# The output accumulator of a decode kernel as two column groups of one bank, with a column-split closing copy and two stores

## The chip, the cores and the metric

The kernel runs on one core of one Trainium2 chip. The metric is device time in microseconds (us) of one execution, as the median of several.

PE is the matmul engine (PEld its weight loads), DVE is VectorE, ACT is ScalarE, POOL is GpSimd, SP is the queue that issues most DMAs. A name like DVEq or SPq is the instruction queue of that engine.

## The reference, cut to what matters

One token for each of four batch rows. A is attention over the last 2048 positions of a cache with 16 key/value heads and 32 query heads; B is a small MLP. The output is 4 rows of 576 numbers.

```python
xn = _layernorm(x)                               # x: (4, 1, 576)
out = x + A(xn, k_cache, v_cache, wq, wo) + B(xn, w1, w2, w3, w4)
# A: q = xn @ wq; softmax(q k^T) v; then  o(4, 4096) @ wo(4096, 576)
# B with S = 1: the shifted terms are zero, so B = xn + gelu(layernorm(xn) @ w3) @ w4,  w4(4608, 576)
```

All three summands end in the same four rows, so the kernel adds them in one accumulator in PSUM, the memory that matmuls write: first `x + xn`, then 32 terms of the wo projection in four groups of eight, then 36 terms of w4. A term is one 128-row slice of the contraction: 128x4 weights against 128x576 moving data.

## The kernel before: the parts that the change touches

The accumulator is one bank of PSUM, and its matmuls take the 576 columns as two halves of `CW` = 288. The kernel before stacks the halves as extra rows. The 4-column weights (`gT`, `op`) lie in a zeroed tile at every second column, 10 wide. A slice of 8 columns that starts at column 1 or at column 0 puts the four batch rows in the even or in the odd output rows and adds zero to the others. Eight rows `(b i)` are thus a contiguous image of the output, and one store writes it.

```python
NI = 2; CW = D // NI                         # 288 columns
OR = NI * B; OW = OR + NI                    # 8 rows, 10-wide padded weights
ROWS = slice(NI - 1, NI - 1 + OR, NI)
gT = cleared([P, NF, OW], "gT")              # zeroed by ACT; data goes to [:, :, ROWS]
op = cleared([P, WOR, OW], "op")
acc = ps_acc.tile([P, CW], F32)              # one PSUM bank
nc.vector.memset(acc[:], 0.0)
second = []

def acc_matmuls(terms):
    for i in range(NI):
        for n, (lhsT, rhs) in enumerate(terms):
            # odd terms go to another bank, at rows 32 to 39, once `second` is set
            to, q, start = (second[0], QD, second[1]) if second and n % 2 else (acc, 0, False)
            nc.tensor.matmul(out=to[q:q + OR, :], lhsT=lhsT[:, NI - 1 - i:NI - 1 - i + OR],
                             rhs=rhs[:, i * CW:(i + 1) * CW], start=start, stop=False, skip_group_check=True)
            if start:
                second[1] = False
```

Before the last wo projection `second` is set. From there even terms go to rows 0 to 7 of `acc` and odd terms to rows 32 to 39 of `acc_odd`, which is another bank. `acc_matmuls` is called for two terms at a time, so neighbours alternate between the banks and run at the same time: in the trace the two of a pair start within 0.01 us of each other, and the pairs are 0.12 us apart at full clock. The w4 matrix arrives in six loads. The last two, of one term each, are summed into `acc` alone, so that ACT can copy `acc_odd` out meanwhile:

```python
W4_PIECES = [0, NFH, NF - 12, NF - 6, NF - 2, NF - 1, NF]     # 0 18 24 30 34 35 36
...
second += [acc_odd, True]
... # o_turn, o_sum, o_spread, o_pick of the last head
o_proj(hl)                                   # 8 terms of wo
mlp_out(*pieces[0]) ... mlp_out(*pieces[3])  # 34 terms of w4
second.clear()
odd = const.tile([OR, CW], F32)
nc.scalar.activation(out=odd[:], in_=acc_odd[QD:QD + OR, :], func=ACT.Copy)
seen = const.tile([1, 1], F32)
nc.vector.tensor_copy(out=seen[:], in_=odd[0:1, 0:1])
for lo, hi in pieces[4:]:                    # terms 34 and 35
    mlp_out(lo, hi)

fin = const.tile([OR, CW], out.dtype)
nc.vector.tensor_tensor(out=fin[:], in0=acc[0:OR, :], in1=odd[:], op=ALU.add)
nc.sync.dma_start(out=o2.rearrange("b (i n) -> (b i) n", i=NI), in_=fin[:])
```

## Time and profile before

| | before |
|---|---|
| median of 3 runs | 211.74 us (211.57 to 211.84) |
| span of the profiled execution | 209.9 us |
| load queue q1 | 87.17 MB, 97.5% of the 16 DMA engines' span |
| PE, DVE busy | 71%, 54% of the span |

The page of the profile, cut to the lines that say what bounds the kernel: busy time of PE, two rows in 40 equal slices of the span (DMA share in tenths, memory traffic), the load queue with its packets, megabytes and share, and the chain of waits by engine.

```profile
span 209.9 us, 2326 instructions
PE 149.1 (71%) x941; PEld 60.2 (29%) x955; DVE 113.7 (54%) x165; ACT 34.4 (16%) x66; POOL 8.9 (4%) x33
...
DMA  8999999999999999999999999999999999999991
GB/s 294 406 403 440 422 428 431 437 425 432 448 429 419 421 437 421 447 418 437 434 425 437 418 426 439 434 423 440 418 431 437 422 433 431 434 428 446 417 399 71
...
q1 hardware_dynamic: 6640, 87.17, 97.5%
...
DMA 52%; PE 24%; DVE 19%; issue 2%; ACT 1%; SPq 0%; DVEq 0%; ACTq 0%
```

The DMA row is 9 in every slice but the first and the last. The stream of loads never pauses, and the last slice is what happens behind it. That slice is where the change acts, so here are its instructions from the timeline (start, duration, engine, line, operation, shapes, count, and in brackets the idle time before and what ended it). In this timeline, lines that don't matter to the point are left out, weight loads above all:

```profile
194.51 1.05 PE L394 MATMUL O<-vn,PT 128*32 128x512 bf16 x16 [0.62 <-DMA vn<-in_A_v_cache_dram]
...
200.70 0.40 PE L183 MATMUL acc<-w_sb,gT 128*8 128x288 bf16 x1 [0.78 <-DMA w_sb<-in_B_w_dram]
...
206.60 0.65 PE L183 MATMUL acc<-w_sb,gT 128*8 128x288 bf16 x4
206.81 0.40 ACT L612 ACTIVATE odd<-acc_odd 8x288 f32<-8x288 f32 x1 [10.46 <-PE acc_odd L183]
207.25 0.14 DVE L614 COPY seen<-odd 1x1 f32<-1x1 f32 x1 [8.54 <-ACT odd L612]
207.32 0.43 DVE L619 TENSOR_TENSOR fin<-acc,odd 8x288 bf16<-8x288 f32 x1
207.78 0.37 SPq L620 DMA_DIRECT2D out_dram<-fin  x1
```

PE starts w4 when its first piece lands. It works off the last four matmuls, two halves of two terms, one after the other from 206.60 and ends at 206.60 + 0.65 = 207.25. Then come one adding copy of 0.43 us, the issue of the store at 207.78, and 2.1 us until the span ends. From the semaphore events of the trace, the six pieces of w4 landed at 200.65, 202.57, 204.69, 206.07, 206.43 and 206.81 us. The end of the kernel can therefore be cut in three:

- **last landing to PE end**: 207.25 - 206.81 = 0.44 us
- **PE end to store issue**: 207.78 - 207.25 = 0.53 us
- **store issue to span end**: 209.89 - 207.78 = 2.11 us

Together they are 3.08 us.

### The profile page before, as it was taken

To read this page: it belongs to the slowest core of one execution; us is meant where nothing else is said; L and a number is where in the kernel's file an instruction comes from. 1 tells how busy PE (TensorE), PEld (TensorE's weight loads), DVE (VectorE), ACT (ScalarE), POOL (GpSimd) and SP (SyncE) were. 2 spreads that over 40 slices of the span, in tenths; PEclk is the share of its full clock that TensorE was granted. 3 is DMA by queue.
4 is the path that set the end of the run, shared out by engine and by line. 5 is a ranking of instruction groups with operands and counts; after the bars stand their busy time and mean duration, and the time that the engine had idled before them with its cause. 6 is when DMAs were issued, how large, how long until landed. Compare 5 with 4: busy or idle time off the path is not lost.

```text
span 209.9 us, 2326 instructions
## 1 busy us (share of the span) xinstructions
PE 149.1 (71%) x941; PEld 60.2 (29%) x955; DVE 113.7 (54%) x165; ACT 34.4 (16%) x66; POOL 8.9 (4%) x33
## 2 busy tenths in 40 slices
PE   0378198699670039649998999659995976898684
PEld 0123032233220013223454333224331312343353
DVE  3611877985910084917507898465949391755200
ACT  7612201021120001111120312110111111113100
POOL 4620000000000000000000300000000000000000
PEclk9999769999996557976999999999997968899969
DMA  8999999999999999999999999999999999999991
GB/s 294 406 403 440 422 428 431 437 425 432 448 429 419 421 437 421 447 418 437 434 425 437 418 426 439 434 423 440 418 431 437 422 433 431 434 428 446 417 399 71
DMA packets 6658, 87.31 MB, mean 416 GB/s; under 512 B 748, under 2 KB 1016, under 8 KB 1656
## 3 DMA queue, kind: packets, MB, share of 16 engines
q1 hardware_dynamic: 6640, 87.17, 97.5%
q8 instruction: 7, 0.11, 0.2%
q10 hardware_dynamic: 8, 0.00, 0.0%
q14 instruction: 3, 0.02, 0.0%
HBM read 87.17 MB, written 0.00 MB: 415 GB/s over the span
## 4 chain that ended last, share of the span: by engine, by line
DMA 52%; PE 24%; DVE 19%; issue 2%; ACT 1%; SPq 0%; DVEq 0%; ACTq 0%
DMA vn<-in_A_v_cache_dram 19%; DMA w_sb<-in_B_w_dram 15%; DVE kt L226 14%; DMA kn<-in_A_k_cache_dram 12%; PE S L342 9%; DMA wq_sb<-in_A_wq_dram 6%; PE acc L183 4%; PE O L394 2%; PE g_ps L460 2%; PE q_ps L286 2%; DVE mx L348 2%; PE S L364 1%; PE oT L407 1%; DVE PT L376 1%; DVE dm L350 1%
## 5 line engine op out<-in xcount | busy, mean ns | idle before, releaser
L342 PE MATMUL S<-kt,qz 128*128 128x512 bf16 x242 | 74.0, 429 | 34.5 <-DVE kt L226 31.3
L226 DVE STREAM_TRANSPOSE kt<-kn 128x2048 int32<-128x2048 int32 x32 | 73.4, 2295 | 26.5 <-DMA kn<-in_A_k_cache_dram 25.0
L342 PEld LDWEIGHTS <-qz 128*128 128x128 bf16 x256 | 24.0, 108 | 63.5 <-issue 46.6
L394 PE MATMUL O<-vn,PT 128*32 128x512 bf16 x256 | 22.9, 400 | 8.4 <-DMA vn<-in_A_v_cache_dram 8.4
L370 ACT ACTIVATE E<-S 128x512 bf16<-128x512 f32 x16 | 9.5, 597 | 97.7 <-PE S L364 97.7
L376 DVE STREAM_TRANSPOSE PT<-E 128x512 bf16<-128x512 bf16 x16 | 11.4, 710 | 15.5 <-ACT E L370 15.5
L401 ACT ACTIVATE O_sb<-O,rd 128x512 f32<-128x512 f32 x16 | 11.0, 686 | 37.1 <-PE O L394 37.1
L394 PEld LDWEIGHTS <-PT 128*32 128x32 bf16 x256 | 5.9, 94 | 29.6 <-issue 28.6
L417 DVE TENSOR_REDUCE on<-oT 128x8 bf16<-128x128 f32 x16 | 4.6, 287 | 16.7 <-PE oT L407 16.6
L348 DVE TENSOR_REDUCE mx<-S 128x1 f32<-128x512 f32 x16 | 10.5, 658 | 1.2 <-PE S L342 1.1
L407 PE MATMUL oT<-ident_w,O_sb 128*128 128x128 f32 x64 | 11.0, 296 | 0.3 <-ACT O_sb L401 0.3
L407 PEld LDWEIGHTS oT<-ident_w,O_sb 128*128 128x128 f32 x64 | 7.0, 146 | 4.6 <-issue 3.9
L183 PE MATMUL acc<-wo_sb,op 128*8 128x288 bf16 x56 | 7.5, 286 | 1.0 <-DVE op L439 1.0
L364 PE MATMUL S<-nm,j_row 8*128 8x512 bf16 x16 | 6.3, 393 | 1.9 <-DVE nm L360 1.7
L183 PE MATMUL acc<-w_sb,gT 128*8 128x288 bf16 x38 | 6.6, 342 | 0.8 <-DMA w_sb<-in_B_w_dram 0.8
L380 PE MATMUL dn<-rs,same_j 128*128 128x1 f32 x32 | 6.4, 268 | 0.0
L380 PEld LDWEIGHTS dn<-rs,same_j 128*128 128x128 f32 x32 | 5.2, 204 | 4.1 <-issue 3.4
L330 PE MATMUL S<-negbig,ohT 4*128 4x512 bf16 x16 | 6.1, 384 | 0.0
L183 PE MATMUL acc_odd<-w_sb,gT 128*8 128x288 bf16 x34 | 6.1, 350 | 0.0
L183 PEld LDWEIGHTS <-op 128*8 128x8 bf16 x64 | 4.6, 87 | 3.2 <-DVE op L439 1.1
L286 PE MATMUL q_ps<-wq_sb,xnT 128*32 128x512 bf16 x40 | 4.5, 630 | 1.3 <-DMA wq_sb<-in_A_wq_dram 1.3
L478 DVE COPY g_x<-gT_ps 128x64 f32<-128x64 f32 (+1 forms) x3 | 0.6, 194 | 8.5 <-PE gT_ps L472 8.5
(93 smaller groups left out, 80.7 us busy)
## 6 DMA issues: line engine op xcount, KB each, us to landing
kn<-in_A_k_cache_dram SPq DMA_DIRECT2D x16, 2048.0 KB, 23.8
vn<-in_A_v_cache_dram SPq DMA_DIRECT2D x16, 2048.0 KB, 25.6
wo_sb<-in_A_wo_dram SPq DMA_DIRECT2D x4, 1152.0 KB, 26.4
w_sb<-in_B_w_dram SPq DMA_DIRECT2D x1, 4608.0 KB, 33.2
wq_sb<-in_A_wq_dram SPq DMA_DIRECT2D x1, 4096.0 KB, 12.8
w_sb<-in_B_w_dram SPq DMA_DIRECT2D x1, 2592.0 KB, 32.2
w_sb<-in_B_w_dram SPq DMA_DIRECT2D x2, 864.0 KB, 34.0
w_sb<-in_B_w_dram SPq DMA_DIRECT2D x2, 576.0 KB, 32.5
```

Source lines behind the costliest of these rows:

```text
L183: nc.tensor.matmul(out=to[q:q + OR, :], lhsT=lhsT[:, NI - 1 - i:NI - 1 - i + OR], rhs=rhs[:, i * CW:(i + 1) * CW], start=start, stop=False ...
L226: nc.vector.transpose(out=kt[:], in_=src)
L286: nc.tensor.matmul(out=q_ps[r][g * QD:(g + 1) * QD, :], lhsT=xnT[:, k, :], rhs=wq_sb[:, col:col + NW], start=(j == 0), stop=False, skip_gr ...
L342: nc.tensor.matmul(out=S_ps[h][:], lhsT=qz[:, z0:z0 + P], rhs=kt[:, ib, c0:c0 + SC, e:2 * QD:2].rearrange("p c k -> p (c k)"), start=False ...
L348: nc.vector.reduce_max(out=mx[:], in_=S_ps[h][:], axis=AX.X)
L364: nc.tensor.matmul(out=S_ps[h][:], lhsT=j_row[:], rhs=st.pop(("nm", h))[:, 0:1].to_broadcast([NJ, NW]), start=False, stop=False, skip_grou ...
L370: nc.scalar.activation(out=E[h][:].rearrange("p c k -> p (c k)"), in_=S_ps.pop(h)[:], func=ACT.Exp, scale=scale, accum_out=rs[:])
L376: nc.vector.transpose(out=PT[h][:], in_=E.pop(h)[:])
L380: nc.tensor.matmul(out=dn[:], lhsT=same_j[:], rhs=st.pop(("rs", h))[:], start=True, stop=True)
L394: nc.tensor.matmul(out=O_ps[h][g * QD:(g + 1) * QD], lhsT=PT[h][:, c, :], rhs=vn[:, :, c, :], start=(s == 0), stop=False, skip_group_check ...
L401: nc.scalar.activation(out=O_sb[h][:], in_=O_ps.pop(h)[:], func=ACT.Copy, scale=st.pop(("rd", h))[:, 0:1])
L407: nc.tensor.transpose(out=oT[:, s, :], in_=o[:, s, :], identity=ident_w[:, s * NJ:s * NJ + P])
```

## The change

The intent is to drop the padded weights and the second bank. Column half `i` of every term goes to partitions 32·i to 32·i+3 of the one accumulator bank, called column group `i` of PE here, so each term is a pair of matmuls that is meant to run at the same time, in the body too. The closing eviction needs no addition, so it is split by columns over DVE and ACT. As the halves are no longer neighbouring rows, there are two stores, on two queues. Two loads of w4 are merged into one.

```diff
-    W4_PIECES = [0, NFH, NF - 12, NF - 6, NF - 2, NF - 1, NF]
+    W4_PIECES = [0, NFH, NF - 6, NF - 2, NF - 1, NF]
...
-    gT = cleared([P, NF, OW], "gT")
-    op = cleared([P, WOR, OW], "op")
+    gT = const.tile([P, NF, B], BF16, name="gT")
+    op = const.tile([P, WOR, B], BF16, name="op")
...
     def acc_matmuls(terms):
-        for i in range(NI):
-            for n, (lhsT, rhs) in enumerate(terms):
-                ... (as printed above)
+        for lhsT, rhs in terms:
+            for i in range(NI):
+                nc.tensor.matmul(out=acc[i * QD:i * QD + B, :], lhsT=lhsT, rhs=rhs[:, i * CW:(i + 1) * CW],
+                                 start=False, stop=False, skip_group_check=True)
...
-    mlp_out(*pieces[0])
-    ... (acc_odd, second, odd, seen: all gone)
+    for lo, hi in pieces:
         mlp_out(lo, hi)
-    fin = const.tile([OR, CW], out.dtype)
-    nc.vector.tensor_tensor(out=fin[:], in0=acc[0:OR, :], in1=odd[:], op=ALU.add)
-    nc.sync.dma_start(out=o2.rearrange("b (i n) -> (b i) n", i=NI), in_=fin[:])
+    fin = const.tile([P, CW], out.dtype)
+    nc.vector.tensor_copy(out=fin[:, 0:CW // 2], in_=acc[:, 0:CW // 2])
+    nc.scalar.activation(out=fin[:, CW // 2:], in_=acc[:, CW // 2:], func=ACT.Copy)
+    for i, eng in enumerate((nc.sync, nc.scalar)):
+        eng.dma_start(out=o2[:, i * CW:(i + 1) * CW], in_=fin[i * QD:i * QD + B, :])
```

Cut: the same reshaping where `op` and `gT` are written, the loops that called `acc_matmuls` for two terms at a time, and the small padded identity `idz` for the first term.

More of the change, by code (lines that the diff above doesn't have):

```diff
@@ L166 @@
     qz = cleared([P, ZP + Hkv * 4 * P], "qz")
-    OR = NI * B
-    OW = OR + NI
-    ROWS = slice(NI - 1, NI - 1 + OR, NI)
-    gT = cleared([P, NF, OW], "gT")
-    op = cleared([P, WOR, OW], "op")
+    gT = const.tile([P, NF, B], BF16, name="gT")
+    op = const.tile([P, WOR, B], BF16, name="op")
     acc = ps_acc.tile([P, CW], F32)
     nc.vector.memset(acc[:], 0.0)
-    second = []
     def acc_matmuls(terms):
-        for i in range(NI):
-            for n, (lhsT, rhs) in enumerate(terms):
-                to, q, start = (second[0], QD, second[1]) if second and n % 2 else (acc, 0, False)
-                nc.tensor.matmul(out=to[q:q + OR, :], lhsT=lhsT[:, NI - 1 - i:NI - 1 - i + OR],
-                                 rhs=rhs[:, i * CW:(i + 1) * CW], start=start, stop=False, skip_group_check=True)
-                if start:
-                    second[1] = False
+        for lhsT, rhs in terms:
+            for i in range(NI):
+                nc.tensor.matmul(out=acc[i * QD:i * QD + B, :], lhsT=lhsT, rhs=rhs[:, i * CW:(i + 1) * CW],
+                                 start=False, stop=False, skip_group_check=True)
     def layernorm(dst_f, dst_bf, src):
@@ L268 @@
     nc.vector.reduce_sum(out=own[:], in_=ident_f[:].rearrange("p (h d) -> p h d", h=WOH), axis=AX.X)
-    idz = const.tile([B, OW], F32)
-    nc.gpsimd.memset(idz[:], 0.0)
-    nc.gpsimd.tensor_copy(out=idz[:, ROWS], in_=ident_f[0:B, 0:B])
     xsum = xn_f
     nc.gpsimd.tensor_tensor(out=xsum[:], in0=xn_f[:], in1=x_bf[:], op=ALU.add)
-    acc_matmuls([(idz[:], xsum)])
+    acc_matmuls([(ident_f[0:B, 0:B], xsum)])
     ln2_bf = part(D, B)
@@ L438, in o_pick @@
         with nc.allow_low_precision("one term is not zero"):
-            nc.vector.reduce_sum(out=op[:, :, ROWS], in_=mk[:].rearrange("p i h b -> p i b h"), axis=AX.X)
+            nc.vector.reduce_sum(out=op[:], in_=mk[:].rearrange("p i h b -> p i b h"), axis=AX.X)
     def o_proj(h):
@@ L443, in o_proj @@
             return
-        for i in range(0, WOR, 2):
-            acc_matmuls([(op[:, i + u, :], wo_tiles[h // WOQ][:, i + u, :]) for u in range(2)])
+        acc_matmuls([(op[:, i, :], wo_tiles[h // WOQ][:, i, :]) for i in range(WOR)])
     G_CHUNKS = [(e, 4 * g, 4) for e in range(2) for g in range(NQD)] + [(e, 16, 2) for e in range(2)]
@@ L486, in mlp_act @@
         nc.gpsimd.tensor_scalar(out=u[:], in0=u[:], scalar1=0.5, scalar2=0.5, op0=ALU.mult, op1=ALU.add)
-        nc.gpsimd.tensor_tensor(out=gT[:, :, ROWS], in0=u[:], in1=xs[:], op=ALU.mult)
+        nc.gpsimd.tensor_tensor(out=gT[:], in0=u[:], in1=xs[:], op=ALU.mult)
     def mlp_out(lo, hi):
         w4 = w_tiles["w4"]
-        for i in range(lo, hi, 2):
-            acc_matmuls([(gT[:, u, :], w4[:, u, :]) for u in range(i, min(i + 2, hi))])
+        acc_matmuls([(gT[:, u, :], w4[:, u, :]) for u in range(lo, hi)])
     order = [("K", 0), ("K", 1), ("K", 2)]
@@ L598 @@
     pieces = list(zip(W4_PIECES, W4_PIECES[1:]))
-    acc_odd = ps_acc.tile([P, CW], F32, tag="g", name="acc_odd")
-    second += [acc_odd, True]
     o_turn(hl)
@@ L605 @@
     o_proj(hl)
-    mlp_out(*pieces[0])
-    mlp_out(*pieces[1])
-    mlp_out(*pieces[2])
-    mlp_out(*pieces[3])
-    second.clear()
-    odd = const.tile([OR, CW], F32)
-    nc.scalar.activation(out=odd[:], in_=acc_odd[QD:QD + OR, :], func=ACT.Copy)
-    seen = const.tile([1, 1], F32)
-    nc.vector.tensor_copy(out=seen[:], in_=odd[0:1, 0:1])
-    for lo, hi in pieces[4:]:
-        mlp_out(lo, hi)
-    fin = const.tile([OR, CW], out.dtype)
-    nc.vector.tensor_tensor(out=fin[:], in0=acc[0:OR, :], in1=odd[:], op=ALU.add)
-    nc.sync.dma_start(out=o2.rearrange("b (i n) -> (b i) n", i=NI), in_=fin[:])
+    for lo, hi in pieces:
+        mlp_out(lo, hi)
+    fin = const.tile([P, CW], out.dtype)
[3 more added lines that the diff above has]
+        eng.dma_start(out=o2[:, i * CW:(i + 1) * CW], in_=fin[i * QD:i * QD + B, :])
 _INS = ['A_x', 'A_k_cache', 'A_v_cache', 'A_wq', 'A_wo', 'B_x', 'B_w1', 'B_w2', 'B_w3', 'B_w4']
```

## The prediction

> **What bounds the kernel now.** The load stream. The page gives queue q1 97.5% of the sixteen DMA engines' span, 87.17 MB at 416 GB/s; DMA leads the chain of waits with 52%. PE (71%) and DVE (54%) wait for data. So a saving in the body is absorbed by slack; only work behind the last loads counts. I read that tail from the timeline from 195 us, and the landings of the w4 pieces from the trace: terms 0-18 at 200.65 us, 18-24 at 202.57, 24-30 at 204.69, 30-34 at 206.07, 34 at 206.43, 35 at 206.81. PE starts w4 at 200.70 on half clock (0.24 us for a pair of matmuls), has the full clock from 204.0 (0.12 us), waits for terms 30-34 until 206.12, and issues its last four matmuls singly from 206.60 at 0.12 us each; term 35 starts at 206.85, just after its landing. PE ends at 207.25, the adding eviction runs 207.32-207.75 (0.435 us), the store is issued at 207.78, and the span ends at 209.9, 2.1 us later.
>
> **What changes.**
> 1. The pairs of even and odd terms in two banks become the two column halves of one term, in two column groups of one bank. I expect the same 0.12 us a pair: the PV matmuls already run four column groups in one bank, sixteen of 512 columns in 1.05 us. [...] Terms 34 and 35, single before, are paired: two slots of 0.12 us saved, but term 35 still waits for its landing at 206.81. Net gain 0.12 us: PE ends near 207.13.
> 2. The output projections in the body, single before (14 matmuls in 1.88 us), halve: about 0.9 us of PE, three times. Absorbed, gain 0.
> 3. Terms 18-30 become one load, landing at 204.69. PE reaches term 18 near 204.5, waits some 0.2 us, then needs 12 x 0.12 us to 206.17, where the next piece has just landed. Cost 0 to 0.1 us.
> 4. Clears of gT and op (0.33 and 0.22 us of ACT near 6.5 us) and idz leave the prologue; q_ps waits until 14.1 us for wq. Gain 0.
> 5. The closing eviction. The built program makes ACT's copy wait for DVE's, so the halves run in series. [...] Estimates: DVE 128x144 about 0.28-0.30 us (from 128x64 at 0.19-0.23), ACT 128x144 about 0.29 us (128x128 took 0.27), plus 0.03-0.05 us of handover: 0.62 against 0.435. Loss 0.19 us. The removed ACT copy (0.40) and DVE copy (0.14) were already hidden, or cost under 0.05 us.
> 6. Two stores on two queues, each half the rows. Both wait for ACT. ACT's issue took 0.55 us at the start, SP's 0.37 now; so the second store may land up to 0.2 us later. Cost 0 to 0.2 us.
>
> Sum: -0.12 + 0.05 + 0.19 - 0.03 + 0.1 = about +0.2 us.
>
> **Prediction.** 211.9 us, 8 in 10 between 211.3 and 212.5. Faster by over 2%: 0.01; within 2%: 0.98; slower: 0.01.
>
> **What would show it.** Step 1: acc pairs 0.12 us apart at full clock. Step 3: a PE wait at term 18. Step 5: ACT's fin copy starting as DVE's ends. Step 6: last store landing against issue. DMA share unchanged.
>
> **What would make it wrong.** One-bank groups running one after the other (up to 4 us more in the tail); the half clock lasting past 206 us, which is chance, in either kernel; a different DMA rate.

## The result, and the profile after

| | before | after |
|---|---|---|
| median, same rounds | 211.79 us (4 runs, 211.57 to 212.02) | 211.92 us (4 runs, 211.62 to 212.03) |
| ratio after to before | | 1.0004, 95% interval 0.9986 to 1.0021 |
| span of the profiled execution | 209.9 us | 210.2 us |

A ratio is the mean time of one kernel's fast runs over that of the other's of the same rounds, so it is not quite the ratio of the medians. The predicted 211.9 us and its range hold.

The same lines of the page, after the change:

```profile
span 210.2 us, 2322 instructions
PE 146.7 (70%) x941; PEld 58.5 (28%) x955; DVE 113.5 (54%) x164; ACT 34.0 (16%) x64; POOL 8.7 (4%) x31
...
DMA  7999999999989999999999999999999999999991
...
q1 hardware_dynamic: 6488, 87.17, 97.3%
...
DMA 50%; PE 26%; DVE 19%; issue 3%; ACT 1%; SPq 0%; ACTq 0%
```

The load stream is what it was: the same bytes, the same share. PE is busy 2.4 us less (1.1 us between the two control traces below), and the span doesn't show it. The last microseconds of the timeline:

```profile
199.88 2.08 PE L177 MATMUL acc<-wo_sb,op 128*4 128x288 bf16 x16 [0.97 <-DVE op L428]
201.75 5.51 PE L177 MATMUL acc<-w_sb,gT 128*4 128x288 bf16 x72
207.30 0.31 DVE L595 CAST fin<-acc 128x144 bf16<-128x144 f32 x1 [7.48 <-PE acc L177]
207.65 0.29 ACT L596 ACTIVATE fin<-acc 128x144 bf16<-128x144 f32 x1 [10.67 <-DVE fin L595]
207.96 0.34 SPq L598 DMA_DIRECT2D out_dram<-fin  x1
207.97 0.27 ACTq L598 DMA_DIRECT2D out_dram<-fin  x1
```

Two things are to be seen. First, ACT's half starts when DVE's half ends (207.30 + 0.31 = 207.61; ACT at 207.65), and the bracket names DVE as what ended ACT's wait. The split eviction takes 207.30 to 207.94, 0.63 us, where the adding copy took 0.43. Second, PE ran all 72 w4 matmuls without one wait for a load, ending at 207.26. It was late: the clock records of the trace give it half clock from 193.4 to 203.6 us in this execution, so w4 began at 201.75 although its first piece had landed at 200.46. That hides the gain that the pairing of the last terms was to bring. The stretches are 0.59, 0.70 and 2.29 us, 3.58 together.

### The profile page after: what moved, and what is told of

Read it like the earlier page. It is cut to its first block, busy times and chain, and to the rows that moved or that the text cites. A ratio compares the mean times of both kernels' runs of the same rounds, so it can differ in the third digit from the quotient of the medians.

```text
span 210.2 us, 2322 instructions
## 1 busy us (share of the span) xinstructions
PE 146.7 (70%) x941; PEld 58.5 (28%) x955; DVE 113.5 (54%) x164; ACT 34.0 (16%) x64; POOL 8.7 (4%) x31
## 4 chain that ended last, share of the span: by engine, by line
DMA 50%; PE 26%; DVE 19%; issue 3%; ACT 1%; SPq 0%; ACTq 0%
DMA vn<-in_A_v_cache_dram 31%; DVE kt L218 14%; DMA kn<-in_A_k_cache_dram 12%; PE S L331 9%; DMA wq_sb<-in_A_wq_dram 6%; PE acc L177 4%; PE O L383 3%; PE g_ps L448 2%; PE oT L396 2%; PE q_ps L275 2%; DVE mx L337 2%; PE S L353 1%; DVE PT L365 1%; DVE dm L339 1%; ACT E L359 1%
## 5 line engine op out<-in xcount | busy, mean ns | idle before, releaser
L383 PE MATMUL O<-vn,PT 128*32 128x512 bf16 x256 | 23.8, 415 | 10.5 <-DMA vn<-in_A_v_cache_dram 10.5
L396 PE MATMUL oT<-ident_w,O_sb 128*128 128x128 f32 x64 | 11.7, 315 | 0.0
L396 PEld LDWEIGHTS oT<-ident_w,O_sb 128*128 128x128 f32 x64 | 7.6, 156 | 4.8 <-issue 4.3
L177 PE MATMUL acc<-wo_sb,op 128*4 128x288 bf16 x64 | 5.5, 324 | 1.0 <-DVE op L428 1.0
L177 PE MATMUL acc<-w_sb,gT 128*4 128x288 bf16 x72 | 5.5, 320 | 0.0
L448 PE MATMUL g_ps<-w_sb,ln2T 128*32 128x512 bf16 (+1 forms) x50 | 4.9, 443 | 0.0
```

What stands on the lines that cost most here:

```text
L177: nc.tensor.matmul(out=acc[i * QD:i * QD + B, :], lhsT=lhsT, rhs=rhs[:, i * CW:(i + 1) * CW], start=False, stop=False, skip_group_check=True)
L383: nc.tensor.matmul(out=O_ps[h][g * QD:(g + 1) * QD], lhsT=PT[h][:, c, :], rhs=vn[:, :, c, :], start=(s == 0), stop=False, skip_group_check ...
L396: nc.tensor.transpose(out=oT[:, s, :], in_=o[:, s, :], identity=ident_w[:, s * NJ:s * NJ + P])
L448: nc.tensor.matmul(out=g_ps[g * QD:(g + 1) * QD], lhsT=ln2T[:, k, :], rhs=rhs, start=(j == 0), stop=False, skip_group_check=True)
```

## The experiments

My theory had six terms: the last two terms are paired (a gain at PE's end), body PE time is slack, the merged load costs little, the cleared tiles were never on the path, the split eviction is serial because its halves share a bank, and the second store costs something. For each that could matter I made a run that tells it from its rival. Each ratio below is to the kernel before, of the same rounds on the same chip. I call "the changed kernel" simply *after*.

### Controls: both kernels once more

One trace of *after* in which PE was at half clock is not enough to read its tail, and one comparison doesn't show the noise. So both kernels ran again, unchanged.

> Control: the kernel before against itself, for the noise of such a comparison and for a second trace of its tail. Ratio 1.000 with an interval of about 0.13% to each side. Tail: last landing to PE end 0.42 to 0.46 us, PE end to store issue 0.53, store issue to span end 2.08 to 2.12.

> Control: the changed kernel once more, for a second trace of its tail. If PE has the full clock during the last microseconds: last landing to PE end 0.32 to 0.36 us instead of the 0.59 of the first profiled run, in which PE ran at half clock until 203.6 us; PE end to store issue 0.70; store issue to span end 2.27 to 2.34. Sum 3.3 to 3.4 us against 3.08 before. Ratio to before 1.0005 to 1.0020.

*Before* against itself gave a ratio of 0.9999 (0.9985 to 1.0013), 211.49 us. *After* gave 1.0018 (1.0005 to 1.0031), 211.68 us (211.61 to 212.18) against 211.50. So in this set the change is slower, by 0.0018 x 211.5 = 0.4 us, with an interval from 0.1 to 0.7 us; two of the five runs, 212.15 and 212.18 us, carry much of that, and by the medians it is 0.2 us. The stretches of *before* came again as 0.46, 0.52 and 2.11 us. Those of *after*, with the half clock over by 197.7 us, were 0.33, 0.70 and 2.28. The timeline of this second trace of *after*:

```profile
200.70 2.37 PE L177 MATMUL acc<-w_sb,gT 128*4 128x288 bf16 x36
204.48 2.41 PE L177 MATMUL acc<-w_sb,gT 128*4 128x288 bf16 x36 [1.41 <-DMA w_sb<-in_B_w_dram]
206.94 0.31 DVE L595 CAST fin<-acc 128x144 bf16<-128x144 f32 x1 [7.27 <-PE acc L177]
207.28 0.29 ACT L596 ACTIVATE fin<-acc 128x144 bf16<-128x144 f32 x1 [10.23 <-DVE fin L595]
207.59 0.34 SPq L598 DMA_DIRECT2D out_dram<-fin  x1
```

At full clock PE waits 1.41 us for the merged piece (terms 18 to 30) and still ends 0.33 us behind the last landing. The tail is 3.31 us against 3.09 in the trace of *before* from the same set: 0.22 us longer, of which PE's end gives -0.13, the eviction +0.18 and the store +0.17 (461, 521 and 2107 ns against 329, 698 and 2282). The prediction had put this sum at +0.2.

### Is the eviction serial, and does that cost 0.17 us? One DVE copy

```diff
-    nc.vector.tensor_copy(out=fin[:, 0:CW // 2], in_=acc[:, 0:CW // 2])
-    nc.scalar.activation(out=fin[:, CW // 2:], in_=acc[:, CW // 2:], func=ACT.Copy)
+    nc.vector.tensor_copy(out=fin[:], in_=acc[:])
```

> The changed kernel with its closing eviction as one VectorE copy of all 288 columns; both stores stay. Theory (the two column halves run in series because they share a bank, so the split costs time): from the end of the last matmul to the store issue 0.50 to 0.55 us, against 0.70 in the changed kernel and 0.53 before; the time falls by about 0.17 us, which is at the edge of what five rounds resolve. Rival (the split overlaps, or the delay is something other than the handover): 0.70 us or more stays, since one copy of 288 columns is not shorter than two halves that overlap.

Ratio 1.0001 (0.9988 to 1.0014), 211.49 us. The eviction lines of its timeline:

```profile
206.93 0.46 DVE L595 CAST fin<-acc 128x288 bf16<-128x288 f32 x1 [7.43 <-PE acc L177]
207.42 0.35 SPq L597 DMA_DIRECT2D out_dram<-fin  x1
```

One copy of 288 columns takes 0.46 us and PE end to store issue is 0.53 us, where the two halves need 0.70. So the theory holds for the stretch; the total, 211.49 us, is too noisy to show 0.17. Giving half of the work to a second engine made the eviction longer, because the second engine waits for the first, and the two copies of 144 columns take 307 and 291 ns where one of 288 takes 458. An estimate for DVE, if its time is linear in the columns: 458 ns for 288 columns and 307 for 144 leave 307 - 151 = 156 ns that don't depend on the columns. ACT's fixed part wasn't measured, but its half takes 290 ns, hardly less.

### Is it the bank? Two banks, evicted at the same time

Here the second half of the columns of each group goes to another bank for the last projection and for w4. What had been summed before is copied out by ACT long before the end and put into the second bank by an identity matmul.

```diff
+            if second:
+                for c, to in enumerate((acc, second[0])):
+                    for i in range(NI):
+                        lo = i * CW + c * (CW // 2)
+                        nc.tensor.matmul(out=to[i * QD:i * QD + B, 0:CW // 2], lhsT=lhsT, rhs=rhs[:, lo:lo + CW // 2], ...)
+                continue
...
-    nc.vector.tensor_copy(out=fin[:, 0:CW // 2], in_=acc[:, 0:CW // 2])
-    nc.scalar.activation(out=fin[:, CW // 2:], in_=acc[:, CW // 2:], func=ACT.Copy)
+    nc.vector.tensor_copy(out=fin[0:2 * QD, 0:CW // 2], in_=acc[0:2 * QD, 0:CW // 2])
+    nc.scalar.activation(out=fin[0:2 * QD, CW // 2:], in_=acc_b[0:2 * QD, :], func=ACT.Copy)
```

> The changed kernel with columns 144 to 287 of each half in a second bank for the last projection and w4 (four matmuls of 144 columns for a term instead of two of 288; what was summed before is copied out and put into the second bank by an identity matmul). VectorE evicts one bank, ScalarE the other. Theory (the shared bank alone puts the halves in series): both copies start within 0.05 us of each other, and the store is issued 0.38 to 0.42 us after the last matmul's end, against 0.70; the time falls by 0.2 to 0.3 us if four short matmuls cost PE no more than two long ones. Rival (the common output tile or the engines' handover puts them in series): ScalarE's copy still starts when VectorE's ends, 0.70 us.

Correct; ratio 1.0001 (0.9989 to 1.0013), 211.51 us. Its timeline at the end:

```profile
207.57 0.28 ACT L611 ACTIVATE fin<-acc_b 64x144 bf16<-64x144 f32 x1 [11.20 <-PE acc_b L182]
207.58 0.30 DVE L610 CAST fin<-acc 64x144 bf16<-64x144 f32 x1 [8.85 <-PE acc_b L182]
207.96 0.27 ACTq L613 DMA_DIRECT2D out_dram<-fin  x1
207.96 0.35 SPq L613 DMA_DIRECT2D out_dram<-fin  x1
```

With a bank each, the copies start 0.01 us apart, both released by PE, though they write the same output tile. PE end to store issue falls from 0.70 to 0.42 us, the upper end of what theory had; the issue follows the later copy by 0.08 us here, behind two waits, instead of 0.03.

So the halves were serial because both were read from one tile in one bank, and not because of the output tile or the engines. The runs show the ordering and its cost (0.70 us against 0.42); why the program orders the two reads isn't shown, as no run here let the two engines read the one bank of the accumulator at the same time. I also built, but didn't run, a variant in which DVE takes rows 0 to 3 and ACT rows 32 to 35 of the one bank. The built program still made ACT wait for DVE. Nor does another bank alone remove the wait: with one accumulator tile that spans two banks, DVE reading the first and ACT the second (also only built), the program again makes ACT wait for DVE's copy. So the built program orders the copies by tile. This run changed tile and bank together and doesn't tell the two apart; whether a split within one bank would pay without the wait is open.

The tail was 3.00 us, 0.31 less than in the control of *after*. The total doesn't resolve that, as *after* didn't run in these rounds. The profiled execution was the slowest of the five (211.96 us), and its loads were late: the first piece of w4 landed at 200.97 us and the last at 207.18, against 200.35 and 206.57 in the control.

### What does the second store cost? One store alone

```diff
-    for i, eng in enumerate((nc.sync, nc.scalar)):
-        eng.dma_start(out=o2[:, i * CW:(i + 1) * CW], in_=fin[i * QD:i * QD + B, :])
+    nc.sync.dma_start(out=o2[:, 0:CW], in_=fin[0:B, :])
```

> The changed kernel with the first of its two stores alone; the other half of the output is not written, so the result is wrong on purpose. Theory (the second store costs 0.18 us, because the span ends with whichever store lands last and the two are in flight together): from store issue to span end 2.1 us, as before the change (2.11), against 2.29 with two. Rival (the 0.18 us come from the store of four rows, or from the issue after ScalarE's copy, not from there being two): 2.29 stays. The total changes by less than five rounds could resolve.

The result was wrong (half of the output isn't written); ratio 1.0004 (0.9990 to 1.0017). With one store, store issue to span end is 2.14 us, and it landed 1.21 us after its issue. With two stores, in all eight fast profiles that have them, ACT's store landed 1.20 to 1.27 us after its issue and SP's 0.18 us after ACT's, 1.37 to 1.45 us after its own issue (which landing is whose, I read from the semaphores that the program waits on). In the second trace of *after*, for instance, both were issued at 207.59 to 207.60, ACT's landed at 208.85 and SP's at 209.03. So the stretch falls by 0.14 us against *after* (2.28). By the landings it is more: SP's store lands 1.21 us after its issue alone and 1.44 beside ACT's in the control, 0.23 us later. The difference of 0.085 us lies behind the landing: in the run with one store SP passes one more wait, for another semaphore, after the store's. Against *before*, whose one store of eight rows landed after 1.25 us, the last landing is 0.19 us later. The theory holds, but not for the reason that the prediction gave.

The prediction expected ACT's issue to be slow (0.55 us at the start of the program), and that issue took 0.27 us, less than SP's 0.34. Why the two landings come one after the other isn't shown. The trace has four packets of 576 bytes for each and four updates of its semaphore as it lands, against eight of both for the one store before, but its packets don't name their DMA engine, so whether the two stores share engines isn't shown either. Nor do the packets show the delay: SP's follow ACT's by 0.03 to 0.05 us in *after* and by 0.10 with two banks, and the landings are 0.18 us apart in both.

### Do the two groups of one bank run at the same time? The tail half by half

The only edit is the order of the w4 matmuls of each piece: all first halves, then all second halves, so that neighbours lie in the same column group.

```diff
-        for lhsT, rhs in terms:
-            for i in range(NI):
+        pairs = [(n, i) for n in range(len(terms)) for i in range(NI)]
+        for n, i in sorted(pairs, key=lambda p: p[1]) if serial else pairs:
```

> The changed kernel with the w4 matmuls of each piece issued half by half, so that neighbours share a column group. The result is the same. Theory (two column groups of one bank really run at the same time, and only because neighbours alternate): PE spends 0.12 us on each matmul instead of on each pair, ends near 211 us instead of 207.3, and the time rises by 3 to 5 us. Rival (the pair spacing of 0.12 us is set by weight loads or by the loads from memory): less than 1 us longer.

Ratio 1.0066 (1.0045 to 1.0087), 212.80 us against 211.57. (One of the six runs took 214.26 us, which lifts the ratio; the medians are 0.6% apart.) The order matters, but by 1.2 us over *before* and by about 1 us over *after*, not by 3 to 5. The total thus falls at the edge of what the rival expected; what decides is the spacing of the matmuls. PE had the full clock throughout:

```profile
198.78 1.15 PE L179 MATMUL acc<-wo_sb,op 128*4 128x288 bf16 x16 [0.97 <-DVE op L430]
200.67 7.34 PE L179 MATMUL acc<-w_sb,gT 128*4 128x288 bf16 x72 [0.74 <-DMA w_sb<-in_B_w_dram]
```

The 16 wo matmuls, still alternating, need 1.15 us, eight pairs; the 72 w4 ones end at 208.00. Starts of w4 matmuls from the trace show why the size was off (first piece: 18 first halves, then 18 second halves):

```
200.666 200.788 200.909 ... 202.133 202.255      14 starts, one by one, 0.122 us apart
202.378 202.384   202.500 202.505   202.623 202.627   202.745 202.749      four pairs
202.872 202.994 203.117 ... 204.342 204.464      14 starts, one by one
```

Within a group a matmul of 288 columns takes 0.122 us. But around a switch of group up to four of them run beside four of the other group: here the last four first halves ran with the first four second halves. PE did not wait until the first group's matmuls were through before it started those of the other group behind them in the program: the first of these started by 202.384 us, before the last three first halves (202.500 us and later). Eighteen and eighteen need 32 slots, not 36, and the whole w4 part 58 slots, not 72. So neighbours of one group do take 0.122 us each, and the rival falls: the weight loads and the loads from memory are the same in both orders. Last landing to PE end grew to 1.23 us. The size that I expected was wrong because I had not counted this run-ahead.

### Is PE time in the body slack?

The first run issues the three body projections half by half, as above.

> The changed kernel with the first three output projections issued half by half (eight matmuls into column group 0, then eight into group 1), so that neighbours share a group; the tail is untouched. Theory (body PE time is slack under the load stream): the sixteen matmuls take about 1.9 us at full clock instead of 1.0, three times, and the time stays within 0.3 us of the changed kernel. Rival (PE time in the body delays buffer release and so the loads): up to 2.7 us longer.

Four of its five executions took 211.60 to 212.01 us; ratio 1.0009 (0.9996 to 1.0022). The fifth, which was the profiled one, took 305.31 us and is left out. In it a matmul of 128x512 took 785 ns on average, against 429 in *before*, and the trace holds no clock records. No other run did that, and I can't explain it. (With PE that slow its work was no longer hidden: the last load landed at 262.28 us and PE ended at 300.55. The slack has a limit.) Because of the run-ahead just seen, this edit also added less PE work than I had planned. A stronger run adds useless work instead:

```diff
         acc_matmuls([(op[:, i, :], wo_tiles[h // WOQ][:, i, :]) for i in range(WOR)])
+        for n in range(4 * WOR if h < Hkv - 1 else 0):
+            nc.tensor.matmul(out=acc[2 * QD:2 * QD + B, :], lhsT=op[:, n % WOR, :], rhs=wo_tiles[h // WOQ][:, n % WOR, 0:CW],
+                             start=False, stop=False, skip_group_check=True)
```

> The changed kernel with 32 useless matmuls of 288 columns behind each of the first three output projections, into rows of the accumulator that nobody reads. At 0.12 us each that is 3.9 us more PE, three times, over four times what the change saved there. Theory (body PE time is slack under the load stream): the time stays within 0.3 us of the changed kernel, and the end of the load stream doesn't move. Rival (body PE time reaches the end through buffers that come free later): 4 us longer or more.

Ratio 1.0013 (1.0000 to 1.0025), 211.80 us: within the two comparisons of *after* (1.0004 and 1.0018). The last piece of w4 landed at 206.69 us, against 206.67 and 206.57 in *after*. Nearly 12 us more of PE work in the body left no mark at the end, so the 0.9 us that the change saved there, three times, couldn't show either. Two reservations: PE began w4 at 201.92 us, later than the 200.45 to 201.01 of the other fast profiles at full clock, which suggests that part of the slack was used up; and the useless work came with a higher mean clock (0.894 to 0.911 in these runs, 0.878 to 0.902 in *after*), so a small loss could be hidden by it. The timeline around the first projection also shows the run-ahead with names on it, since the useless matmuls have their own line, L435, and come behind all sixteen of L177 in the program:

```profile
103.37 0.78 PE L177 MATMUL acc<-wo_sb,op 128*4 128x288 bf16 x10
103.87 0.28 PE L435 MATMUL acc<-wo_sb,op 128*4 128x288 bf16 x1
103.98 0.29 PE L177 MATMUL acc<-wo_sb,op 128*4 128x288 bf16 x2
103.99 0.28 PE L435 MATMUL acc<-wo_sb,op 128*4 128x288 bf16 x1
104.10 0.29 PE L177 MATMUL acc<-wo_sb,op 128*4 128x288 bf16 x2
104.11 0.29 PE L435 MATMUL acc<-wo_sb,op 128*4 128x288 bf16 x1
104.23 0.29 PE L177 MATMUL acc<-wo_sb,op 128*4 128x288 bf16 x2
104.23 3.35 PE L435 MATMUL acc<-wo_sb,op 128*4 128x288 bf16 x26
```

The first L435 starts at 103.87, before six matmuls of L177 that stand ahead of it in the program.

### What does set the end? More bytes

```diff
             nc.sync.dma_start(out=t[:, lo:hi, :], in_=src[:, lo - e * NFH:hi - e * NFH, :])
+            if lo == 0:
+                extra = wop.tile([P, WOR, D], BF16, tag="wo", name="extra")
+                nc.sync.dma_start(out=extra[:, 0:4, :], in_=src[:, 0:4, :])
```

> The changed kernel with four terms of w4 (590 KB) loaded a second time into a buffer that nobody reads, ahead of the last pieces. Theory (the end of the load stream sets the end of the kernel): at the 433 GB/s of the late slices this takes 1.36 us, all landings behind it and the span move by that, and the tail behind the last landing stays as it was. Rival (PE or the issue of loads sets the end): less than 0.7 us longer.

Ratio 1.0093 (1.0071 to 1.0116), 213.19 us, 1.5 us above *after* of the same rounds (211.68). The last landing moved from 206.57 to 208.11 us, by 1.54, and the tail behind it stayed at 3.35 us (3.31 in *after*). So 0.7% more bytes cost 0.7% more time, while 12 us of PE work cost nothing that shows. The 1.54 us are more than the 1.36 expected, but 0.16 of them were there before the extra bytes: the first piece of w4, ahead of them in the queue, landed at 200.51 us against 200.35. From there to the last landing it is 7.60 us against 6.22, 1.39 more.

### The merged load

> The changed kernel with terms 18 to 30 of w4 as two loads, as before the change. Theory (merging them costs 0 to 0.1 us): with the full clock PE waits at term 24 or 30 for a landing and ends 0.33 to 0.36 us after the last landing in either layout; the time moves by less than 0.1 us, unresolved. Rival (the larger piece delays PE to the end): PE ends at least 0.1 us earlier after the last landing than the 0.33 us that a five-piece kernel showed at full clock.

The edit puts `NF - 12` back into `W4_PIECES` of *after*. Ratio 1.0017 (1.0002 to 1.0033), as *after* in the control. Last landing to PE end is 0.33 us, as with five pieces in the control. The merged load costs nothing that shows; four terms and two single ones still follow it.

### A version meant to beat both

If the terms add up, the best closing keeps the eight contiguous rows and the one store of *before* and splits the columns over two groups and two banks.

```diff
+                for c in range(2):
+                    to = second[0] if second and c else acc
+                    lo = i * CW + c * (CW // 2)
+                    nc.tensor.matmul(out=to[c * QD:c * QD + OR, :], lhsT=lhsT[:, NI - 1 - i:NI - 1 - i + OR],
+                                     rhs=rhs[:, lo:lo + CW // 2], start=False, stop=False, skip_group_check=True)
...
-    nc.vector.tensor_tensor(out=fin[:], in0=acc[0:OR, :], in1=odd[:], op=ALU.add)
+    nc.vector.tensor_copy(out=fin[:, 0:CW // 2], in_=acc[0:OR, :])
+    nc.scalar.activation(out=fin[:, CW // 2:], in_=acc_b[QD:QD + OR, :], func=ACT.Copy)
```

> A version meant to beat both. The kernel before (eight output rows in one column group, one store) with the columns of each half split in two: columns 0 to 143 in column group 0 of one bank, 144 to 287 in group 1 of a second bank, so that the matmuls alternate between groups, VectorE and ScalarE evict a bank each at the same time, and one store follows. Theory (the parts add up): last landing to PE end 0.33 us, PE end to store issue 0.43, store issue to span end 2.11, together 2.87 us, against 3.08 before and 3.58 in the changed kernel's profiled run. In the total 0.2 us less than before, at most just resolved; a different clock or landing can hide it. Rival (some part of the closing is set by something else): one of the three stretches stays as it was.

Correct. Its timeline at the end:

```profile
207.12 0.28 ACT L615 ACTIVATE fin<-acc_b 8x144 bf16<-8x144 f32 x1 [10.92 <-PE acc_b L185]
207.15 0.30 DVE L614 CAST fin<-acc 8x144 bf16<-8x144 f32 x1 [8.60 <-PE acc_b L185]
207.53 0.36 SPq L616 DMA_DIRECT2D out_dram<-fin  x1
```

The stretches were 0.34, 0.48 and 2.09 us, 2.90 together, the shortest tail of all, and 0.2 us shorter than *before*. The middle one is 0.05 us longer than expected: as with two banks, the issue follows the later copy by 0.08 us. The total was 211.57 us (211.40 to 211.82) against 211.59, ratio 1.0001 (0.9988 to 1.0013). The tail is shorter where the trace can see it; that the kernel is faster is not shown, and an interval of 0.13% to each side, 0.3 us, couldn't show 0.2.

### The stretches side by side

All times from one trace each, in us. The first column names PE's clock while it worked on w4.

| kernel | clock | last landing | to PE end | to store issue | to span end | sum |
|---|---|---|---|---|---|---|
| before | half until 204.0 | 206.81 | 0.44 | 0.53 | 2.11 | 3.08 |
| before, control | full | 206.77 | 0.46 | 0.52 | 2.11 | 3.09 |
| after | half until 203.6 | 206.67 | 0.59 | 0.70 | 2.29 | 3.58 |
| after, control | full | 206.57 | 0.33 | 0.70 | 2.28 | 3.31 |
| one DVE copy | full | 206.56 | 0.33 | 0.53 | 2.29 | 3.15 |
| two banks | full | 207.18 | 0.36 | 0.42 | 2.22 | 3.00 |
| one store | full | 206.73 | 0.33 | 0.70 | 2.14 | 3.17 |
| closing meant to beat both | half until 202.0 | 206.72 | 0.34 | 0.48 | 2.09 | 2.90 |

## Why the prediction was right, point by point

The time, 211.92 us against 211.9, and the verdict "same" were right. Agreement to 0.02 us is luck, as runs scatter by 0.4. What carries weight is that most terms of the sum were each found at about their predicted size.

1. **Pairing in one bank, -0.12 us at PE's end.** Right, -0.13 between the two controls at full clock. In the profiled execution of the comparison it was absent, since half clock made PE late: 0.59 instead of 0.33 us. The prediction had named the half clock as chance, but only if it lasted past 206 us; it ended at 203.6 and was enough, because it had also delayed the start of w4. Whether it also made the slower runs of *after* (212.15 and 212.18 in the control) I can't say, as only one execution of each was read.
2. **The halved body projections are worth nothing.** Right; nearly 12 us of useless PE work cost nothing that shows.
3. **The merged load, 0 to 0.1 us.** Right at the lower end. The predicted wait at term 18 was there in the control at full clock (1.41 us of PE idle), longer than predicted, and harmless.
4. **The cleared tiles are off the path.** Right as far as seen: q_ps starts with the landing of wq, at 14.1 us before and 13.9 after. There was no run for it alone.
5. **Serial eviction, +0.19 us.** Right: 0.63 us against 0.43; PE end to store issue 0.70 against 0.53. A second tile in a second bank removes it. (The prediction's 0.27 us for ACT were of copies of 4x128 and 8x128 in the trace before, not 128x128; the 0.29 came true all the same.) The -0.03 us for the two removed copies were about 0.02: the closing copy starts 0.06 us after PE's end in the control of *before* and 0.04 in that of *after*.
6. **The second store, 0 to 0.2 us.** The size was within the range, 0.17 between the controls, where the sum had 0.1; the reason was wrong. It was not ACT's issue that was slow. SP's store landed 0.18 us behind ACT's, though both were issued within 0.01 us.

So where did the expected gain of a leaner accumulator go? The large part, PE time in the body and the cleared tiles, lay beside a load stream that sets the pace. The small part, 0.13 us at PE's end, was given back by the serial eviction and the second store. The net is a slightly longer tail, which the first comparison couldn't resolve and the second just could.

## What to carry to other kernels

Splitting one PSUM eviction over two engines paid here only when each read its own tile in its own bank (0.42 us from PE's end to the store issue); from one tile the halves ran one after the other, and the split was slower (0.70) than a single copy (0.53). In a kernel that loads without a pause, cut the time behind the last landing into PE's end, eviction and store, and judge a change of the closing by these three alone. For PE, let neighbouring matmuls fall in different column groups; one bank served as well as two here (0.12 us a pair in either, against 0.12 us for each matmul among neighbours of one group).

## What the traces show of the chip

- Across column groups matmuls did not start in program order. With useless matmuls behind the projection, one started at 103.87 us before six earlier ones of the other two groups, which started from 103.98 on, and in the half-by-half tail four matmuls of the second group ran beside the last four of the first. It was four matmuls at each switch of group read here: the first two of the half-by-half tail and the one behind the first projection.
- A pair of 288-column matmuls in two groups took 0.122 us at full clock, whether in one bank or in two, and neighbours within a group took 0.122 us each.
- The clock records of PE hold 0.5 or 1.0. In the trace of *before*, w4 pairs are 0.24 us apart at 0.5 and 0.12 us at 1.0. A small part at half clock can matter: at the tail of *after* it was worth 0.26 us (0.59 against 0.33 in its control at full clock), 0.1% of the span and more than the change's whole effect on the tail, 0.22.
- With only this one core at work, its loads moved 415 GB/s over the span of *after*.
- Two small stores on two queues, issued together, land 0.18 us apart in all eight fast profiles that have two.
